# A hand-written opening for a fused pooled-attention and mixture-of-experts kernel

## The chip, the cores and the metric

The kernel runs on one core of one Trainium2 chip. It is one launch; the time is device microseconds of that core. The engines are TensorE (PE in the profile, its weight loads PEld), VectorE (DVE), ScalarE (ACT), GpSimd (POOL) and SyncE (SP), which here issues nearly all transfers. Each engine works through its own instructions in the order in which they stand in its program and waits at an instruction until what it reads is there and what it overwrites has been read.

## The reference, cut to what matters

```python
B, H, S, D = 8, 8, 576, 64                     # q, k, v: [B, H, S, D] f32
k_p = k.reshape(B, H, 72, 8, D).mean(axis=3)   # pooled by 8
v_p = v.reshape(B, H, 72, 8, D).mean(axis=3)
attn = softmax(q @ k_p.T / 8)                  # [B, H, 576, 72]
x = (attn @ v_p) as [4608, 512]                # tokens x (heads, D)
g_idx = argmax(x @ w_group)                    # 4 groups
e_idx = argmax(x @ w_expert[g_idx])            # 4 experts in each
h = maximum(x @ w1[g, e], 0)                   # 512 -> 1024
out = gate_g * gate_e * (h @ w2[g, e])         # 1024 -> 512
```

The routing picks one expert out of 16 for each token; the two gates are the softmax weights of the picks.

## The kernel before

The eight batches go through one after the other, as a software pipeline: while the expert products of batch b run on TensorE, the other engines prepare the attention of batch b+1 and fetch q, k and v of batch b+2. Of each batch one "main" expert is worked on densely for all 576 tokens; the few tokens that went elsewhere are left for a loop behind the last batch. For every batch but the first, the main expert is counted out of the routing. Batch 0 has to start before any routing is known, so its main expert is guessed: `guess_x` (lines 476 to 484) takes the mean of pooled v as a stand-in for x, `guess_e` (line 487 on) multiplies it with the router weights and takes the largest group and expert. The result, `me` (line 471), is read into a register by SyncE, and only then can the eight transfers of that expert's w1 and w2 be issued (line 548).

The order of all instructions is written out by hand in four strings of pieces: `START`, `FIRST`, `STEADY` and `LAST`. `run` (line 916) goes through a string and calls the piece's method, which emits its instructions on their engines in that order. A piece is `who.method:arguments`. The letter a is the attention of the batch at hand, n that of the next, x that of the one after it; m is its experts' part, w the next one's, t a helper. `START` and then `FIRST` are batch 0; nothing else in the program comes before them but the making of constants.

The pieces of the opening, with what they do:

- `load_k:u`, `load_v:u`, `load_r`, `load_q:c`: transfers from HBM; k and v come in two big tiles each (u = 0, 1) and a rest of 64 rows each, which lie in one tile `rem` (v in partitions 0 to 63, k in 64 to 127). q comes in five chunks c of 128 tokens (the last has 64). `load_wr` fetches the router weights, on ScalarE's queue.
- `kr`, `vr`, `rr` (lines 225 to 237): the sums over 8 neighbours, of a k tile, a v tile, the rest. A letter says on which engine: r is one reduction on VectorE, p three additions on GpSimd (line 217 on).
- `kt` and `kta`: transpose pooled k on TensorE, copy it out of PSUM on ScalarE as `kT`. `qt`, `qta`: the same for a chunk of q.
- `sc`, `mx`, `sb`, `ex`, `su_`, `nm`, `pt`: for a chunk, the scores on TensorE (tile `sc`, of which there are two buffers), the row maximum and the subtraction on VectorE, the exponential on ScalarE, the sums and their reciprocal on VectorE, the scaling on GpSimd, the transposition into `pT` on VectorE.
- `rep`, `repa`, `repd`: pooled v repeated along partitions by TensorE, and copied out as `v4` by ScalarE and, masked, as `v5` by VectorE.
- `av:c0:c1`, `ava`, `avd`: the product with v for chunks c0 to c1, and its two copies, a rounded one by ScalarE and the rounding's rest by VectorE (tile `xt`).
- `turn_wr`, `put_wr`: the router weights transposed into `wr`.
- `m.load:1:j`, `m.split:1:j`, `m.spd:1:j`: a quarter j of w1 is fetched, rounded on ScalarE (line 555), and the rounding's rest taken on VectorE (v, line 561) or GpSimd (p, line 565).
- `m.up:f:hf` (line 567): twelve matrix products, one block of 128 columns of w1 with half of the tokens; blocks 2f' and 2f'+1 need quarter f'. `m.ua`, `m.upd` copy it out.
- `t.warm:z` (line 906): z products of a tile of ones with itself, whose result nobody reads.

A tile of a pool with a single buffer, as `rem`, can be filled for the next batch only when its readers are done; SyncE then waits at that transfer, and every transfer behind it in its queue waits too.

Of the kernel before, what the change touches and what calls it, by code (L numbers as in the profile page):

```python
# [46 lines left out]
a.ex:4 m.ua:5:0 n.load_qb:0 a.su_:2 a.nm:2:p a.su_:4 m.ua:3:0 a.nm:4:p m.upd:2:0 a.pt:2 m.split:1:0 a.pt:4 n.rr:r m.ua:4:0 x.load_r:k a.av:2:4  # L47
m.upd:5:0 a.ava:2:2 m.spd:1:3:v a.ava:2:0 n.qb:0 a.avd:2:2 m.upd:3:0 n.kt n.kta m.upd:4:0 a.ava:2:1 n.load_v:0 m.up:6:0 a.ava:2:3 m.up:7:0 n.qb:2
a.avd:2:3 m.ua:7:0 a.avd:2:0 n.sc:2 m.spd:1:0:p m.load:2:3 n.sc:0 a.avd:2:1 n.mx:2 n.sb:2 m.upd:7:0 n.mx:0 n.vr:1:p n.qb:1 x.load_r:v m.ua:6:0
m.load:2:1 m.up:7:1 m.load:2:0 m.split:2:3 n.vr:0 m.up:1:0 m.up:0:0 n.ex:2 n.sc:1 m.upd:6:0 a.rt n.qb:4 m.load:2:2 n.su_:2 n.rep n.sb:0 m.ua:7:1  # L50
m.upd:7:1 x.load_qb:3 n.mx:1 n.nm:2:p m.ua:0:0 n.pt:2 m.spd:2:3:p m.ua:1:0 m.upd:0:0 n.sb:1 m.up:6:1 n.qb:3 m.upd:1:0 n.repa:0 a.route n.ex:0
m.split:2:2 x.load_k:0 x.load_qb:0 m.up:3:1 x.load_k:1 m.ua:6:1 m.ua:3:1 n.ex:1 x.load_v:1 m.split:2:0 n.su_:0 a.count m.up:1:1 n.repa:1 m.up:2:1
m.upd:6:1 n.sc:3 n.repd:1 m.split:2:1 n.sc:4 m.ua:2:1 n.su_:1 m.up:0:1 a.keep_x m.ua:1:1 n.repd:0 n.nm:0:p m.upd:3:1 n.nm:1:p m.upd:2:1 m.spd:2:1:p
m.up:5:1 m.up:4:1 n.mx:4 n.pt:0 m.upd:1:1 n.mx:3 m.spd:2:0:p n.pt:1 m.down:0 n.sb:3 n.sb:4 m.ua:5:1 n.ex:3 m.ua:0:1 n.ex:4 m.ua:4:1 m.upd:5:1
# [906 lines left out]
```

## Time and profile before

| | |
|---|---|
| three runs | 554.21, 553.89, 552.15 us (median 553.89) |
| the profiled execution | 552.38 us, of which its span is 550.7 us |
| instructions | 15235 |
| TensorE busy | 525.7 us (95% of the span) |
| VectorE, GpSimd, ScalarE busy | 360.2, 276.3 and 211.7 us |
| granted TensorE clock, mean of the span | 0.981 |

The page divides the span into 40 slices of 13.8 us. TensorE is busy in nine tenths of nearly every slice; the first has 3 tenths, the second 7 and the third 8, and the last 5. The granted clock, in tenths of full speed, reads 9, 6, 7 in the first three slices, 9 from the fourth to the last but one, and 8 in the last. What the table calls busy is the time in which an instruction was in an engine, whatever clock it had; a product at clock 0.50 counts twice the time of the same product at 1.00.

### The profile page before, as it was taken

The page shows a single profiled execution, that of the slowest core. Times are in us where ns is not written, and L with a number is a line of the kernel's source. Part 1 is how long each engine was busy: PE and PEld are TensorE (multiplying, and loading weights), DVE is VectorE, ACT ScalarE, POOL GpSimd, SP SyncE. Part 2 cuts the span into 40 slices and gives each one's busy share as a digit, 9 for nine tenths or more (in the row PEclk, how much of TensorE's full clock was granted, in tenths as well). Part 3 has the DMA queues.
Part 4 walks back from the last instruction along what each step waited for, and adds up shares of the span by engine and source line. Part 5 has one row for each costly group of instructions (what it writes and reads, how often), then busy time and mean ns, then how long its engine had stood idle before and what let it go on. Part 6 is the DMA issues. An engine that isn't in the chain of part 4 may idle for free.

```text
span 550.7 us, 15235 instructions
## 1 busy us (share of the span) xinstructions
PE 525.7 (95%) x6218; PEld 468.5 (85%) x6218; DVE 360.2 (65%) x940; ACT 211.7 (38%) x402; POOL 276.3 (50%) x259
## 2 busy tenths in 40 slices
PE   3789999999999999999999999999999999999995
PEld 2689987789888998899888998899788988899874
DVE  4788898757755875768755775768756763447520
ACT  2253523445315353355225452354225442344111
POOL 3437386035933578056934578056924554085400
PEclk9679999999999999999999999999999999999998
DMA  9778651591418805492619714496518200544801
...
DMA packets 115649, 81.32 MB, mean 148 GB/s; under 512 B 73562, under 2 KB 92250, under 8 KB 115192
## 3 DMA queue, kind: packets, MB, share of 16 engines
...
## 4 chain that ended last, share of the span: by engine, by line
PE 88%; DMA 4%; DVE 3%; issue 1%; ACT 1%; SPq 1%; POOL 0%; ACTq 0%; POOLq 0%
PE mm L578 36%; PE mm L617 29%; PE sc L374 5%; PE mm L622 5%; PE sc L320 4%; DMA sw<-in_moe_w_dram 2%; PE tp L408 1%; DMA rem<-in_k_dram 1%; DMA ht<-in_moe_w_expert_dram 1%; PE mm L597 1%; PE sc L244 1%; PE mm L910 1%; PE tp L374 1%; DVE su L342 0%; SPq L548 0%
## 5 line engine op out<-in xcount | busy, mean ns | idle before, releaser
L578 PE MATMUL mm<-xt,w 128*128 128x256 f32 (+1 forms) x1536 | 211.7, 297 | 0.9 <-DVE ht L588 0.9
L578 PEld LDWEIGHTS mm<-xt,w 128*128 128x128 f32 x1536 | 205.8, 189 | 3.5 <-ACT ht L583 1.0
L617 PE MATMUL mm<-w,ht 128*128 128x512 f32 x744 | 177.4, 393 | 0.0
L617 PEld LDWEIGHTS mm<-w,ht 128*128 128x128 f32 x744 | 137.9, 188 | 31.2 <-issue 2.5
L565 POOL TENSOR_TENSOR w<-sw,w 128x512 fp32r<-128x512 f32 x94 | 122.6, 1328 | 82.8 <-ACT w L555 80.7
L349 POOL TENSOR_TENSOR p<-p,su 128x576 f32<-128x576 f32 (+1 forms) x40 | 45.8, 1150 | 133.9 <-DVE su L344 126.7
L583 ACT ACTIVATE ht<-mm 128x320 fp32r<-128x320 f32 (+1 forms) x128 | 49.4, 408 | 108.4 <-PE mm L578 108.3
L588 DVE SCALAR_TENSOR_TENSOR ht<-mm,ht 128x256 fp32r<-128x256 f32 (+1 forms) x192 | 60.0, 343 | 39.9 <-ACT ht L583 38.7
L555 ACT CAST w<-sw 128x1024 fp32r<-128x1024 f32 x64 | 66.0, 1043 | 20.5 <-DMA sw<-in_moe_w_dram 16.0
L630 ACT ACTIVATE y<-mm,gm 128x512 f32<-128x512 f32 x31 | 21.3, 687 | 70.0 <-PE mm L617 63.6
L399 POOL TENSOR_TENSOR sw<-xt 128x640 f32<-128x640 f32 (+1 forms) x28 | 40.0, 1463 | 7.2 <-DVE xt L392 7.2
L342 DVE TENSOR_REDUCE su<-p 128x8 f32<-128x576 f32 (+1 forms) x40 | 29.7, 743 | 15.1 <-ACT p L337 15.0
L309 DVE STREAM_TRANSPOSE qT<-q 128x512 f32<-128x512 f32 x35 | 24.6, 702 | 22.7 <-PE sc L320 16.1
L218 POOL TENSOR_TENSOR kv<-kv 128x512 f32<-128x512 f32 x21 | 29.9, 1425 | 10.0 <-DMA kv<-in_v_dram 7.6
L374 PE MATMUL sc<-pT,v 32*64 32x128 f32 (+11 forms) x1560 | 31.0, 290 | 2.6 <-DVE m L493 1.1
L326 DVE TENSOR_REDUCE mx<-sc 128x8 f32<-128x576 f32 (+1 forms) x40 | 29.4, 736 | 6.3 <-PE sc L320 6.3
L355 DVE STREAM_TRANSPOSE pT<-p 128x576 f32<-128x576 f32 (+1 forms) x40 | 30.8, 769 | 3.1 <-POOL p L349 3.1
L337 ACT ACTIVATE p<-p 128x576 f32<-128x576 f32 (+1 forms) x40 | 27.4, 684 | 13.1 <-DVE p L333 8.3
L622 PE MATMUL mm<-w,ht 128*128 128x512 f32 x128 | 32.3, 396 | 0.0
L374 PEld LDWEIGHTS sc<-pT,v 32*64 32x64 f32 (+3 forms) x1560 | 27.4, 139 | 5.6 <-issue 3.2
L561 DVE TENSOR_TENSOR w<-sw,w 128x1024 fp32r<-128x1024 f32 x17 | 24.3, 1428 | 9.2 <-ACT w L555 9.2
L333 DVE TENSOR_TENSOR p<-sc,mx 128x576 f32<-128x576 f32 (+1 forms) x40 | 29.8, 747 | 0.2
(217 smaller groups left out, 480.7 us busy)
## 6 DMA issues: line engine op xcount, KB each, us to landing
...
```

What stands on the lines that cost most here:

```text
L218: add(out=a[..., 0:256], in0=a[..., 0:256], in1=a[..., 256:512], op=ALU.add)
L349: (nc.vector if eng == "v" else nc.gpsimd).tensor_tensor(out=pf, in0=pf, in1=bc(sf, SP), op=ALU.mult)
L355: nc.vector.transpose(out=s.pT[0:n, :, 32 * c:32 * c + 32], in_=s.p[c].rearrange("p u x s -> p (u x s)").rearrange("p (b i) -> p b i", i=3 ...
L374: nc.tensor.matmul(to[64 * x:64 * x + 64], lhsT=w, rhs=s.pT[e, k, 32 * c0:32 * c0 + n], start=(z == 0), stop=(z == 2))
L399: nc.gpsimd.tensor_tensor(out=x, in0=a, in1=b, op=ALU.add)
L555: nc.scalar.copy(out=wh, in_=raw)
L565: nc.gpsimd.tensor_tensor(out=wl[:, p], in0=raw[:, p], in1=wh[:, p].bitcast(F32), op=ALU.subtract)
L578: nc.tensor.matmul(ps[:, 0:n], lhsT=l[:, kc, fs], rhs=xt[:, r, kc, sl], start=(kc == 0 and i == 0), stop=(kc == 3 and i == 2))
L583: nc.scalar.activation(out=s.ht[f][:, o:o + n], in_=s.pu[f, hf][:, 0:n], func=AF.Relu)
L588: stt(out=ht[:, at:at + hi - lo], in0=ps[:, lo - o:hi - o], scalar=0.0, in1=ht[:, lo:hi].bitcast(F32), op0=ALU.max, op1=ALU.subtract)
L617: nc.tensor.matmul(ps, lhsT=s.ht[f][:, 640 * l + o:640 * l + o + 128], rhs=s.w[2, f // 2][r][:, f % 2, :], start=(i == 0), stop=(i == 23))
L622: nc.tensor.matmul(ps, lhsT=s.ht[f][:, 512:640], rhs=s.w[2, f // 2][r][:, f % 2, :], start=(i == 0), stop=(i == 15))
```

## The change

Both strings of the opening, `START` and `FIRST`, are written anew, and three methods learn to do their work in parts. The later strings are as they were. The order within `FIRST` differs only at its beginning.

```diff
 START = """
-a.load_k:1:w a.load_k:0:w a.load_q:0 a.qt:0 a.load_r:k a.load_r:v a.load_q:1 a.kr:0:r a.kr:1:p a.load_v:0 a.load_v:1 a.rr:r a.qta:0 a.load_q:3 a.kt
-n.load_r:v t.load_wr a.kta a.qt:1 a.load_q:4 a.vr:0:r a.sc:0 a.mx:0 t.turn_wr a.qta:1 a.vr:1:p a.sc:1 a.load_q:2 t.warm:2 a.sb:0 n.load_r:k a.ex:0
-n.load_k:0 a.mx:1 t.put_wr a.sb:1 a.su_:0 a.qt:3 a.ex:1 a.rep a.guess_x a.nm:0:p a.su_:1 a.repd:1 a.repa:1 a.nm:1:p n.load_v:1 a.pt:0 a.repa:0 a.qt:2
...
-a.su_:3 t.warm:4 a.nm:3:p a.qta:4 t.warm:7
+t.load_wr t.warm:8 a.load_k:1:w a.load_k:0:w a.load_q:0 a.load_r:k a.load_q:1 a.qt:0 a.kr:0:r a.kr:1:p a.load_r:v a.load_v:0 a.load_v:1 a.qta:0
+a.load_q:3 a.kt a.rr:r:k a.ktail a.kta a.qt:1 a.load_q:4 a.load_q:2 a.rr:p:v a.qta:1 a.sc:0 a.mx:0 a.vr:0:r:0 a.vr:0:p:1 n.load_r:v a.sc:1 a.sb:0
+t.turn_wr a.vr:1:r:0 a.vr:1:p:1 a.ex:0 a.mx:1 t.put_wr a.qt:3 n.load_r:k n.load_k:0 a.sb:1 a.ex:1 a.guess_x n.load_v:1 n.load_k:1 a.su_:0 a.nm:0:p
+a.su_:1 a.rep a.nm:1:p a.pt:0 a.pt:1 a.repd:1 a.repa:1 a.repa:0 a.repd:0 a.guess_e a.qta:3 m.load:1:1 m.load:1:2 m.load:1:3 m.load:1:0 a.av:0:1 a.qt:2
...
+a.sb:3 a.ex:3 n.load_qb:3 n.load_qb:1 a.sc:2 a.mx:2 a.su_:3 a.qta:4
 """
 FIRST = """
-m.split:1:3 a.mx:2 m.up:2:0 n.load_qb:2 m.split:1:2 m.ua:2:0 a.sc:4 a.sb:2 t.warm:8 m.spd:1:2:p m.up:3:0 a.pt:3 m.up:4:0 m.up:5:0 a.ex:2 a.mx:4 a.sb:4
...
+m.up:2:0 a.nm:3:p m.split:1:2 n.load_qb:2 m.ua:2:0 m.up:3:0 a.sb:2 m.spd:1:2:p a.sc:4 m.split:1:3 a.pt:3 m.up:4:0 m.up:5:0 a.ex:2 a.mx:4 a.sb:4 a.ex:4
...
-        def rr(s, eng="r"):
-            s.rp = wk.tile([128, D], F32, name="rp")
-            s.total(s.rp, s.rem, eng)
+        def rr(s, eng="r", part=None):
+            if s.rp is None:
+                s.rp = wk.tile([128, D], F32, name="rp")
+            r = {None: slice(0, 128), "v": slice(0, 64), "k": slice(64, 128)}[part]
+            s.total(s.rp[r], s.rem[r], eng)
...
+            if t is None:
+                s.total(s.vp[:, 2 * u:2 * u + 2, :], s.v[u], eng)
+            else:
+                s.total(s.vp[:, 2 * u + t, :], s.v[u][:, t], eng)
...
+        def ktail(s, ps=None):
+            if ps is None:
+                ps = s.tk2 = ps_m.tile([128, 512], F32, name="mm")
+            for a in range(2):
+                nc.tensor.matmul(ps[64 * a:64 * a + 64, 256:320], lhsT=s.rp[64:128], rhs=ident[64:128, 64:128], start=True, stop=True)
```

So the sum over the rest is now two sums: k's half on VectorE, v's half on GpSimd, and `ktail`, the transposition of the first, is a piece of its own. Each v tile is summed by two engines, one half each. In the program after, lines below 230 stand 5 to 8 lines further down (a score product is L328 and not L320, a product of ones L918 and not L910, an up block L586 and not L578).

On TensorE the program of before begins with these rows (q transposed, k transposed, the k rest, q again, scores of chunk 0, router weights, scores of chunk 1, ones, q):

```order
L298 MATMUL mm<-ident,q 128x128 x4
L273 MATMUL tp<-ident,kp 64x128 x8
L264 MATMUL mm<-ident,rp 64x64 x2
L298 MATMUL mm<-ident,q 128x128 x4
L320 MATMUL sc<-kT,qT 64x72 x16
L900 MATMUL mm<-ident,ht 128x20 x4
L320 MATMUL sc<-kT,qT 64x72 x16
L910 MATMUL mm<-ones 128x128 x2
L298 MATMUL mm<-ident,q 128x128 x4
```

The program of after has in the same place, with eight products of ones in front:

```order
L918 MATMUL mm<-ones 128x128 x8
L306 MATMUL mm<-ident,q 128x128 x4
L277 MATMUL tp<-ident,kp 64x128 x8
L283 MATMUL mm<-ident,rp 64x64 x2
L306 MATMUL mm<-ident,q 128x128 x4
L328 MATMUL sc<-kT,qT 64x72 x32
L908 MATMUL mm<-ident,ht 128x20 x4
L306 MATMUL mm<-ident,q 128x128 x4
```

The router weights' products no longer stand between the scores of chunk 0 and those of chunk 1, and the two products of ones behind them are gone.

Behind the first product with v, TensorE had before (last chunk of q, scores of chunks 3 and 2, ones, one up block, scores of chunk 4, ones, three up blocks):

```order
L298 MATMUL mm<-ident,q 128x64 x4
L320 MATMUL sc<-kT,qT 64x72 x32
L910 MATMUL mm<-ones 128x128 x11
L578 MATMUL mm<-xt,w 128x256 x12
L320 MATMUL sc<-kT,qT 64x72 x8
L910 MATMUL mm<-ones 128x128 x8
L578 MATMUL mm<-xt,w 128x256 x36
```

In the program after these rows read:

```order
L306 MATMUL mm<-ident,q 128x128 x4
L306 MATMUL mm<-ident,q 128x64 x4
L328 MATMUL sc<-kT,qT 64x72 x32
L586 MATMUL mm<-xt,w 128x256 x24
L328 MATMUL sc<-kT,qT 64x72 x8
L586 MATMUL mm<-xt,w 128x256 x24
```

The transposition of q's chunk 2 has come behind the product with v, both groups of ones are gone, and a second up block stands ahead of the last scores. The next row is in both programs the second product with v, `av:2:4`.

On VectorE the sums and the softmax of chunks 0 and 1 stood so before:

```order
L215 TENSOR_REDUCE kp<-w 128x128
L215 TENSOR_REDUCE rp<-rem 128x64
L215 TENSOR_REDUCE vp<-kv 128x128
L326 TENSOR_REDUCE mx<-sc 128x8
L333 TENSOR_TENSOR p<-sc,mx 128x2x4x72
L326 TENSOR_REDUCE mx<-sc 128x8
L333 TENSOR_TENSOR p<-sc,mx 128x2x4x72
```

And after:

```order
L215 TENSOR_REDUCE kp<-w 128x128
L215 TENSOR_REDUCE rp<-rem 64x64
L334 TENSOR_REDUCE mx<-sc 128x8
L215 TENSOR_REDUCE vp<-kv 128x64
L341 TENSOR_TENSOR p<-sc,mx 128x2x4x72
L215 TENSOR_REDUCE vp<-kv 128x64
L334 TENSOR_REDUCE mx<-sc 128x8
L341 TENSOR_TENSOR p<-sc,mx 128x2x4x72
```

The single reduction of v's first tile has become two reductions, of a half of the first tile and a half of the second, and they stand among the softmax steps.

## Rows read from the trace of the kernel before

**Rows 1.** Stretches: start:end, width, busy of PE, PEld, DVE, ACT, POOL, PEclk, DMA
```profile
13.00:16.00 3.00, 0.09 (x1) 0.12 (x2) 2.84 (x3) 0.09 (x1) 1.07 (x1) 0.76 1.26 161
...
21.00:23.00 2.00, 2.00 (x24) 1.81 (x23) 1.89 (x5) 0.15 (x1) 1.59 (x2) 0.91 0.93 293
...
33.00:35.00 2.00, 2.00 (x14) 1.86 (x11) 1.97 (x4) 1.23 (x3) 0.00 (x0) 0.50 0.96 297
35.00:37.00 2.00, 2.00 (x20) 2.00 (x19) 1.90 (x5) 1.07 (x2) 0.76 (x1) 1.00 1.23 291
```

**Rows 2.** The same view, all that comes behind the opening
```profile
60.00:550.70 490.70, 479.72 (x5290) 426.34 (x5282) 315.05 (x849) 189.91 (x358) 247.70 (x215) 1.00 0.48 142
```

**Rows 3.** Chain that ended last, its start: start us, us, what
```profile
2.35 7.28 DMA rem<-in_k_dram
...
9.65 6.12 DMA ht<-in_moe_w_expert_dram
```

**Rows 4.** Timeline, TensorE: start us, us, engine, line, op, out<-in, shapes [idle before <-releaser]
```profile
7.59 1.09 PE L298 MATMUL mm<-ident,q 128*128 128x128 f32 x4 [7.59 <-DMA q<-in_q_dram]
...
15.91 0.63 PE L900 MATMUL mm<-ident,ht 20*128 20x20 f32 x4 [2.93 <-DMA ht<-in_moe_w_expert_dram]
...
18.65 1.06 PE L298 MATMUL mm<-ident,q 128*128 128x128 f32 x4
...
25.68 3.23 PE L374 MATMUL sc<-pT,v 32*64 32x64 f32 x192 [1.12 <-DVE m L493]
...
30.93 2.29 PE L320 MATMUL sc<-kT,qT 64*64 64x72 f32 x64 [1.41 <-DVE xt L392]
...
36.51 1.68 PE L578 MATMUL mm<-xt,w 128*128 128x256 f32 x12
38.11 0.72 PE L320 MATMUL sc<-kT,qT 64*64 64x72 f32 x16
...
45.21 2.55 PE L374 MATMUL sc<-pT,v 32*64 32x96 f32 x192
```

**Rows 5.** Timeline, VectorE
```profile
10.33 1.01 DVE L215 TENSOR_REDUCE rp<-rem 128x64 f32<-128x512 f32 x1 [2.30 <-DMA rem<-in_v_dram]
...
17.78 0.76 DVE L326 TENSOR_REDUCE mx<-sc 128x8 f32<-128x576 f32 x1 [1.90 <-PE sc L320]
18.57 0.76 DVE L333 TENSOR_TENSOR p<-sc,mx 128x576 f32<-128x576 f32 x1
...
24.55 0.29 DVE L261 TENSOR_TENSOR v<-sc,mask 128x128 f32<-128x128 f32 x1 [1.60 <-ACT v L253]
...
25.84 1.16 DVE L497 TENSOR_TENSOR cr<-dg 128x16 f32<-128x16 f32 x1
...
27.45 0.15 DVE L471 TENSOR_SCALAR me<-ct 128x1 int32<-128x1 f32 x1
...
33.78 1.22 DVE L561 TENSOR_TENSOR w<-sw,w 128x1024 fp32r<-128x1024 f32 x1
...
38.88 0.75 DVE L326 TENSOR_REDUCE mx<-sc 64x8 f32<-64x576 f32 x1 [0.67 <-PE sc L320]
...
44.38 0.77 DVE L355 STREAM_TRANSPOSE pT<-p 64x576 f32<-64x576 f32 x1 [0.35 <-POOL p L349]
```

**Rows 6.** Timeline, GpSimd
```profile
14.93 1.26 POOL L218 TENSOR_TENSOR kv<-kv 128x512 f32<-128x512 f32 x1 [7.56 <-DMA kv<-in_v_dram]
...
22.13 1.15 POOL L349 TENSOR_TENSOR p<-p,su 128x576 f32<-128x576 f32 x1 [0.41 <-DVE su L344]
25.70 1.27 POOL L218 TENSOR_TENSOR kv<-kv 128x512 f32<-128x512 f32 x1 [2.42 <-DMA kv<-in_k_dram]
...
38.01 2.50 POOL L565 TENSOR_TENSOR w<-sw,w 128x512 fp32r<-128x512 f32 x2 [0.61 <-ACT w L555]
```

**Rows 7.** Timeline, ScalarE
```profile
32.24 1.04 ACT L555 CAST w<-sw 128x1024 fp32r<-128x1024 f32 x1 [1.75 <-DMA sw<-in_moe_w_dram]
```

**Rows 8.** Timeline, SyncE's queue
```profile
28.64 2.11 SPq L548 DMA_DIRECT2D sw<-in_moe_w_dram x4
```

More of the change, by code (lines that the diff above doesn't have):

```diff
@@ L47 @@
[L47 to L54, printed above, removed]
@@ L55 @@
-m.upd:0:1 n.su_:4 m.spd:2:2:p n.nm:4:p m.upd:4:1 a.gex n.su_:3 n.nm:3:p m.down:12 x.kr:1:p n.pt:4 m.down:13 n.pt:3 n.av:0:4 x.load_qb:2 x.load_qb:1
-n.ava:0:1 x.kr:0:r x.load_v:0 m.down:1 x.rr:r a.gates n.ava:0:4 n.ava:0:0 n.ava:0:3 n.ava:0:2 n.avd:0:4 n.avd:0:0 x.vr:1:p n.avd:0:3 m.da:4 n.avd:0:2
-m.down:2 n.xr:0 m.down:9 n.xr:3 x.kt x.qb:0 n.ava:0:5 n.avd:0:1 n.avd:0:5 x.kta n.xr:2 m.down:6 x.vr:0:r x.sc:0 n.xr:1 n.rt x.rep x.mx:0 x.sb:0
-n.route x.repa:0 x.repd:1 m.down:10 n.main_expert w.load:1:0 x.ex:0 m.da:0 n.gex w.load:1:1 x.su_:0 m.down:11 x.repa:1 w.load:1:3 m.down:3 m.down:4
@@ L59 @@
-w.load:1:2 x.qb:1 x.repd:0 m.down:7 n.gates w.load:2:1 w.split:1:0 m.da:3 w.load:2:0 x.nm:0:p m.down:5 w.spd:1:0:v n.keep_x x.pt:0 w.split:1:1 m.da:1
-m.down:8 m.da:2 w.spd:1:1:v
+m.up:2:0 a.nm:3:p m.split:1:2 n.load_qb:2 m.ua:2:0 m.up:3:0 a.sb:2 m.spd:1:2:p a.sc:4 m.split:1:3 a.pt:3 m.up:4:0 m.up:5:0 a.ex:2 a.mx:4 a.sb:4 a.ex:4
+m.ua:5:0 n.load_qb:0 a.su_:2 a.nm:2:p a.su_:4 m.ua:3:0 a.nm:4:p m.upd:2:0 a.pt:2 m.split:1:0 a.pt:4 n.rr:r m.ua:4:0 x.load_r:k a.av:2:4 m.upd:5:0
+a.ava:2:2 m.spd:1:3:v a.ava:2:0 n.qb:0 a.avd:2:2 m.upd:3:0 n.kt n.kta m.upd:4:0 a.ava:2:1 n.load_v:0 m.up:6:0 a.ava:2:3 m.up:7:0 n.qb:2 a.avd:2:3
@@ new lines @@
+m.ua:7:0 a.avd:2:0 n.sc:2 m.spd:1:0:p m.load:2:3 n.sc:0 a.avd:2:1 n.mx:2 n.sb:2 m.upd:7:0 n.mx:0 n.vr:1:p n.qb:1 x.load_r:v m.ua:6:0 m.load:2:1
+m.up:7:1 m.load:2:0 m.split:2:3 n.vr:0 m.up:1:0 m.up:0:0 n.ex:2 n.sc:1 m.upd:6:0 a.rt n.qb:4 m.load:2:2 n.su_:2 n.rep n.sb:0 m.ua:7:1 m.upd:7:1
+x.load_qb:3 n.mx:1 n.nm:2:p m.ua:0:0 n.pt:2 m.spd:2:3:p m.ua:1:0 m.upd:0:0 n.sb:1 m.up:6:1 n.qb:3 m.upd:1:0 n.repa:0 a.route n.ex:0 m.split:2:2
+x.load_k:0 x.load_qb:0 m.up:3:1 x.load_k:1 m.ua:6:1 m.ua:3:1 n.ex:1 x.load_v:1 m.split:2:0 n.su_:0 a.count m.up:1:1 n.repa:1 m.up:2:1 m.upd:6:1 n.sc:3
@@ new lines @@
+n.repd:1 m.split:2:1 n.sc:4 m.ua:2:1 n.su_:1 m.up:0:1 a.keep_x m.ua:1:1 n.repd:0 n.nm:0:p m.upd:3:1 n.nm:1:p m.upd:2:1 m.spd:2:1:p m.up:5:1 m.up:4:1
+n.mx:4 n.pt:0 m.upd:1:1 n.mx:3 m.spd:2:0:p n.pt:1 m.down:0 n.sb:3 n.sb:4 m.ua:5:1 n.ex:3 m.ua:0:1 n.ex:4 m.ua:4:1 m.upd:5:1 m.upd:0:1 n.su_:4
+m.spd:2:2:p n.nm:4:p m.upd:4:1 a.gex n.su_:3 n.nm:3:p m.down:12 x.kr:1:p n.pt:4 m.down:13 n.pt:3 n.av:0:4 x.load_qb:2 x.load_qb:1 n.ava:0:1 x.kr:0:r
+x.load_v:0 m.down:1 x.rr:r a.gates n.ava:0:4 n.ava:0:0 n.ava:0:3 n.ava:0:2 n.avd:0:4 n.avd:0:0 x.vr:1:p n.avd:0:3 m.da:4 n.avd:0:2 m.down:2 n.xr:0
@@ L61 @@
+m.down:9 n.xr:3 x.kt x.qb:0 n.ava:0:5 n.avd:0:1 n.avd:0:5 x.kta n.xr:2 m.down:6 x.vr:0:r x.sc:0 n.xr:1 n.rt x.rep x.mx:0 x.sb:0 n.route x.repa:0
+x.repd:1 m.down:10 n.main_expert w.load:1:0 x.ex:0 m.da:0 n.gex w.load:1:1 x.su_:0 m.down:11 x.repa:1 w.load:1:3 m.down:3 m.down:4 w.load:1:2 x.qb:1
+x.repd:0 m.down:7 n.gates w.load:2:1 w.split:1:0 m.da:3 w.load:2:0 x.nm:0:p m.down:5 w.spd:1:0:v n.keep_x x.pt:0 w.split:1:1 m.da:1 m.down:8 m.da:2
+w.spd:1:1:v
 """
@@ L263, in kt @@
         def kt(s):
-            tail = lambda ps: [nc.tensor.matmul(ps[64 * a:64 * a + 64, 256:320], lhsT=s.rp[64:128], rhs=ident[64:128, 64:128], start=True, stop=True) for a in range(2)]
             ps = s.tk = ps_t.tile([128, 512], F32, name="tp")
@@ L268, in kt @@
                     nc.tensor.transpose(out=ps[:, 128 * z:128 * z + 128], in_=flat(s.kp[:, 2 * z:2 * z + 2, :]), identity=ident)
-                tail(ps)
+                s.ktail(ps)
                 return
@@ L273, in kt @@
                     nc.tensor.matmul(ps[64 * y:64 * y + 64, 128 * g:128 * g + 128], lhsT=s.kp[:, 2 * (g % 2) + g // 2], rhs=ident, start=True, stop=True)
-            ps = s.tk2 = ps_m.tile([128, 512], F32, name="mm")
-            tail(ps)
+        def ktail(s, ps=None):
[3 more added lines that the diff above has]
+                nc.tensor.matmul(ps[64 * a:64 * a + 64, 256:320], lhsT=s.rp[64:128], rhs=ident[64:128, 64:128], start=True, stop=True)
         def kta(s):
```

6 lines of the change are left out of this document (2 added, 4 removed).

## The prediction

> **What bounds the kernel now.** I read the stretches first. Behind the opening TensorE is busy for 479.72 of 490.70 us at full clock [rows 2]: there the kernel is as long as TensorE's work, the change leaves that work alone, and time can only come out of the opening, or be lost in it. The number that decides is therefore when TensorE starts the second product with v (`av:2:4`), 45.21 us before [rows 4]: the four up blocks that stand ahead of it in both programs are then done, and the rest is the same program.
>
> Next the chain of waits. It goes at the start through two landings: k's rest, issued at 2.35, lands at 9.63, and the router weights, issued at 9.65, land 6.12 us later [rows 3]. TensorE stands for 2.93 us at the products of these weights, until 15.91, and the scores of chunk 1 stand behind them [rows 4]. So VectorE gets chunk 1's maximum only at 17.78 [rows 5].
>
> Then the timelines, for the chain from there to the guess: chunk 1's subtraction ends at 19.33, its scaling on GpSimd runs from 22.13, VectorE waits 1.60 us before the second piece of `v5`, and `me` is ready at 27.60 [rows 5, 6]. SyncE issues the first expert transfer at 28.64, 1.04 later [rows 8], ScalarE's rounding begins at 32.24, 3.6 after the issue [rows 7], VectorE's part ends at 35.00 [rows 5]. The first up block starts at 36.51, behind eleven products of ones [rows 4].
>
> Last the clock. TensorE's granted clock is 1.00 up to some point in 13 to 16 us, in which TensorE is nearly idle, and has a mean of 0.76 there; it is back in 21 to 23, low again at 33 to 35, and 1.00 from 35 on [rows 1]: the levels of 1.2 and 2.4 GHz. The opening is worked off largely at the low one.
>
> **The change part by part**, made against the profiled execution's own time, 552.38 us.
>
> *Router weights first.* Their transfer goes from behind the first copy of q to the first place of ScalarE's queue; it lands long before it is used, and the 2.93 us go. Price: 40 KB in front of k; at the 161 GB/s of 13 to 16 us [rows 1] that is 0.25 us, and I take 0, since VectorE's next tie is v.
>
> *The rest in two halves.* VectorE waited for v's half too and began at 10.33 [rows 5]; k's half landed at 9.63 [rows 3]. That is 0.7 us earlier for kT. Scores of chunk 0 ended before at 12.98 (15.91 less 2.93 [rows 4]), so now at 12.3 to 13.0; I take 12.6.
>
> *v by two engines.* A reduction of 512 columns took 1.01 us [rows 5]. VectorE now does: maximum of chunk 0 (0.76) to 13.4, first half of v to 14.4, subtraction (0.76) to 15.2, second half (v's second tile landed at 14.93 [rows 6]) to 16.2, maximum of chunk 1 to 17.0, subtraction to 17.8. Before it ended at 19.33 [rows 5]: 1.5 us gained. GpSimd's halves have no row; half a tile costs between half and all of the 2.6 us of a whole one (14.93 to 17.5 [rows 6]), so pooled v is complete between 16.2 and 17.5, and either is hidden, since the second scaling comes only after it.
>
> *Guess ahead of the repeated sums.* From chunk 1's subtraction to its scaling it took 2.8 us (19.33 to 22.13 [rows 5, 6]): now 20.6. Scaling 1.15 [rows 6], to 21.75. From the piece of `v5` to `me` VectorE needed 3.05 us (24.55 to 27.60 [rows 5]), which holds the transposition and the choice of the expert; `v5`'s other piece, with twice the columns of the 0.29 us one, is estimated at 0.4. That gives 25.2. The wait of 1.60 us is gone, as `v4` no longer comes between.
>
> In these 3.05 us one addition of 16 columns takes 1.16 us while its neighbour takes 0.15, and GpSimd's sum of 25.70 to 26.97 runs beside it [rows 5, 6]. That sum waits for a transfer (2.42 us idle before it); the transfers are as many as before, so it stays near 25.7 and the guess no longer meets it. So the addition costs some 0.2 and `me` is ready at 24.2; were it slow for another reason, 25.2. I take 24.2, 3.4 us earlier. The Trainium skill, "SBUF — State Buffer", section "Who interferes with whom", says that a VectorE instruction with two SBUF inputs and a GpSimd one that reads SBUF exclude each other; by it 24.2 stands, and without it 25.2 would.
>
> *Up blocks ahead of the last scores, no products of ones.* Issue at 24.2 + 1.04 = 25.25; rounding from 28.85 to 29.9. The product with v starts with `v5` at 23.2 and takes 3.23 [rows 4], 2.5 us earlier than before; scores of chunks 3 and 2, before at 30.93, start at 28.4 and take 2.29 [rows 4], to 30.7. VectorE's maximum (29.5 to 30.3) and its part of the weights (1.22 [rows 5]) end at 31.5. So the first up block starts at 31.5 instead of 36.51. But it starts on the low clock: the eleven products of ones, which before kept TensorE busy from 30.93 until the clock rose at 35.0 [rows 1, 4], are gone. A block took 1.60 us at full clock (36.51 to 38.11 [rows 4]), so 3.2 at half. If the clock rises again 4.1 us after TensorE went to work without a break, at 35.6, then 1.28 blocks are done, the other 0.72 take 1.15, and the scores of chunk 4 start at 36.75, before 38.11. Their maximum starts at 37.5, before 38.88 [rows 4, 5].
>
> Bounds: no rise until both blocks are done, 31.5 + 6.4 = 37.9, maximum at 38.7, gain 0.2. Full clock at once, 34.7; then VectorE is late next. Between the weights' part and this maximum it took 3.9 us (35.00 to 38.88 [rows 5]) and has one subtraction (0.76) more in between, so 36.1: gain 2.8. I take 1.4, the value with the rise that the trace shows.
>
> From that maximum to the last transposition VectorE has the same instructions in both programs, 6.27 us (38.88 to 45.15 [rows 5]). `av:2:4` starts at 43.8 instead of 45.21.
>
> *Products of ones in front.* They lie in the first 7.59 us, in which TensorE waits for q [rows 4]. The four transpositions at 7.59 take 1.09, as at 18.65 on the low clock (1.06) [rows 4]. If the eight products raise the clock, k's transposition is done earlier, and k's rest (above) is late next: between 0 and 0.3 us at the scores, and 0 behind v's second landing. I take 0.
>
> *Sum.* 552.38 - 1.4 = 551.0 on the profiled execution. It lies 1.5 us under the median of 553.89; the four times shown (552.15, 552.38, 553.89, 554.21) have a mean of 553.16, 0.8 above it. I add these 0.8: 551.8.
>
> **Rivals.**
>
> *The clock falls ahead of the second product with v (slower).* Behind the last scores TensorE now has two up blocks only. They need GpSimd's part (2.50 us, before to 40.51 [rows 6], now to about 37.8), take 3.2 and end at 41.0; the product can't start before 43.8. That is 2.8 us of idleness where before eight products of ones and a third block stood. An idle stretch of 2.93 us took the clock down before [rows 1, 4]. A low stretch lasts long: 0.76 in 13 to 16 and 0.91 in 21 to 23 put its ends at 14.6 and 21.4, 6.8 us [rows 1]. In work that TensorE bounds [rows 2] half of that is lost: 3.4 - 1.4 = 2.0 slower, 554.4, with the 0.8 555.2. Against it: the idle stretch has dense work on its left, and the one of 13 to 16 had light work there. It decides if the clock drops between 41 and 46 us. The Trainium skill, "TensorE: Matmul & The Clock Gate", section "HAM oscillation — how this bites in real kernels", warns of just this: idleness between bursts puts the following burst on the low clock; the trace agrees with its 2.93 us, and no run here shows it at this place.
>
> *The up blocks find the clock high, or the chain is quicker.* The gain is then the 2.8 of VectorE's bound: 552.38 - 2.8 + 0.8 = 550.4. For it: TensorE has scores just before. Against: these scores, from 30.93 on, had not raised the clock before 35 [rows 1, 4].
>
> *The order brings nothing (no change).* Two q transfers are now issued earlier, and VectorE waits for v's second tile where GpSimd did. Each 1 us by which this lands behind 15.2 moves everything behind; at 16.6 the 1.4 are gone: 553.2. For it: 7.56 us of GpSimd's waiting was for this tile [rows 6]. Against: the q transfers stand behind it in the queue.
>
> **How the numbers follow.** Forecast 0.43, clock falls 0.25, quick chain 0.17, nothing 0.15. A difference of 0.5%, 2.8 us, is about what a measurement of this kernel tells from no change: faster is below 551.1, slower above 556.7. The forecast lies 0.7 above the first and counts to it with four parts in ten (0.17), the quick chain nearly whole (0.15), the rest with 0.01: 0.33. Slower is the fall of the clock with little gain: 0.07. The same: 0.60. The range reaches from the quick chain's 550.4 less the 1 us by which runs of one program differ from their mean, 549.4, to the falling clock's 555.0.
>
> **What would show it.** No wait of TensorE before the router weights' products, and chunk 1's maximum at 16 to 17 us; `me` at 24 to 25.2; first expert transfer at 25 to 26.5; the first up block at 31 to 32.5, its products twice as long as those before the second product with v; that product at 43 to 44.5, with 2 to 3 us of idleness before it. The forecast is wrong if v's second tile lands behind 16 us, if `av:2:4` starts before 42, or if a stretch behind 43 us shows a clock under 1.00.

## The result, and the profile after

Seven runs of each program on one chip: 556.59 us after (555.0 to 558.51), 553.58 before (551.01 to 555.63). The ratio is 1.0068, its 95% interval 1.0042 to 1.0095: by it the kernel is slower by 0.7%; the medians lie 3.0 us apart. The profiled execution of after took 558.51 us and is the longest of its seven; that of before took 552.38. So the two traces lie 6.1 us apart, and the traces tell where time goes, the ratios how much.

TensorE's timeline of after answers to [rows 4] (start us, us, engine, line, op, out<-in, shapes, count, idle before and its releaser):

```profile
12.15 1.48 PE L328 MATMUL sc<-kT,qT 64*64 64x72 f32 x64
...
24.18 3.41 PE L382 MATMUL sc<-pT,v 32*64 32x64 f32 x192 [2.00 <-ACT v L258]
28.47 1.63 PE L306 MATMUL mm<-ident,q 128*128 128x128 f32 x8 [0.87 <-issue]
30.03 2.20 PE L328 MATMUL sc<-kT,qT 64*64 64x72 f32 x64
...
33.28 5.27 PE L586 MATMUL mm<-xt,w 128*128 128x256 f32 x23 [0.54 <-DVE w L569]
38.48 0.72 PE L328 MATMUL sc<-kT,qT 64*64 64x72 f32 x16
39.13 1.70 PE L586 MATMUL mm<-xt,w 128*128 128x256 f32 x12
...
43.76 1.77 PE L586 MATMUL mm<-xt,w 128*128 128x256 f32 x12 [2.94 <-DVE ht L596]
45.66 4.12 PE L382 MATMUL sc<-pT,v 32*64 32x96 f32 x192
...
50.74 5.22 PE L586 MATMUL mm<-xt,w 128*128 128x256 f32 x24
55.88 1.23 PE L328 MATMUL sc<-kT,qT 64*64 64x72 f32 x64
```

Four things are to be seen. The router weights no longer hold the scores up: all 64 records run in one piece from 12.15. The first up blocks start 3.2 us earlier than in [rows 4], but take 5.27 us for 23 records, and the last scores behind them start 0.37 us later than before, at 38.48. Then TensorE stands still for 2.94 us ahead of up block 5. And from `av:2:4` on (45.66, 0.45 us later than before) each product takes longer: 4.12 us where [rows 4] have 2.55.

The stretches answer to [rows 1] (start:end, width, busy time of PE, PEld, DVE, ACT, POOL, granted clock, DMA share, GB/s):

```profile
13.00:16.00 3.00, 1.21 (x36) 1.03 (x36) 2.97 (x4) 0.53 (x1) 2.69 (x7) 1.00 1.26 199
21.00:23.00 2.00, 1.19 (x6) 1.07 (x6) 1.23 (x3) 0.05 (x1) 0.80 (x1) 0.50 0.96 354
33.00:35.00 2.00, 1.72 (x8) 1.73 (x9) 1.86 (x4) 1.01 (x3) 0.00 (x0) 0.50 1.24 284
35.00:37.00 2.00, 2.00 (x11) 2.00 (x11) 1.45 (x4) 1.85 (x3) 0.96 (x1) 0.50 0.93 86
...
39.00:45.00 6.00, 3.06 (x30) 2.78 (x25) 5.24 (x11) 0.68 (x1) 2.96 (x3) 1.00 0.67 108
...
46.00:55.00 9.00, 9.00 (x218) 8.37 (x203) 5.58 (x11) 3.61 (x10) 7.44 (x8) 0.50 0.79 203
```

At 35 to 37 us, where the clock was 1.00 before [rows 1], it is 0.50. From 39 to 45 TensorE works 3.06 of 6 us; then it is busy without a break from 46 to 55 at clock 0.50, 1.2 GHz. That stretch costs 1.57 us in `av:2:4` (4.12 less 2.55) and 2.09 in the two blocks behind it (5.22; before they took 3.13). From the start of `av:2:4` to the scores behind these blocks it is 10.22 us where it was 6.17, so 4.05 in all. The scores at 55.88 stood at 51.38 before: of the 6.1 us, 4.5 are lost by then; where the rest goes is not followed here. Behind 60 us TensorE is again busy nearly throughout, as in [rows 2]:

```profile
60.00:556.80 496.80, 484.37 (x5403) 430.73 (x5401) 319.69 (x859) 190.75 (x360) 250.44 (x217) 1.00 0.46 140
```

VectorE's timeline answers to [rows 5]:

```profile
17.09 0.76 DVE L341 TENSOR_TENSOR p<-sc,mx 128x576 f32<-128x576 f32 x1
...
24.16 0.29 DVE L266 TENSOR_TENSOR v<-sc,mask 128x128 f32<-128x128 f32 x1 [1.25 <-ACT v L258]
...
24.79 0.17 DVE L505 TENSOR_TENSOR cr<-dg 128x16 f32<-128x16 f32 x1
...
25.41 0.15 DVE L479 TENSOR_SCALAR me<-ct 128x1 int32<-128x1 f32 x1
...
32.01 1.22 DVE L569 TENSOR_TENSOR w<-sw,w 128x1024 fp32r<-128x1024 f32 x1
...
39.24 0.75 DVE L334 TENSOR_REDUCE mx<-sc 64x8 f32<-64x576 f32 x1 [1.24 <-PE sc L328]
...
43.35 0.36 DVE L596 SCALAR_TENSOR_TENSOR ht<-mm,ht 128x256 fp32r<-128x256 f32 x1
```

GpSimd scales chunk 1 from 20.65 ([rows 6]: 22.13), the guess is ready at 25.56 (27.60 before), SyncE issues the first expert transfer at 26.61 ([rows 8]: 28.64), ScalarE rounds from 30.12 ([rows 7]: 32.24), and VectorE's part of the weights ends at 33.2 (35.00 before). All of this is lost again by 39.24, when the maximum of chunk 4 starts, 0.36 us later than before. The last row is what up block 5 waits for: its PSUM buffer is that of block 2, and `m.upd:2:0`, which empties it, stands behind all sums of chunk 4.

### The profile page after: what moved, and what is told of

Read it like the earlier page. It is cut to its first block, busy times and chain, and to the rows that moved or that the text cites. A ratio compares the mean times of both kernels' runs of the same rounds, so it can differ in the third digit from the quotient of the medians.

```text
span 556.8 us, 15189 instructions
## 1 busy us (share of the span) xinstructions
PE 530.9 (95%) x6192; PEld 472.7 (85%) x6192; DVE 360.2 (65%) x941; ACT 211.9 (38%) x402; POOL 278.3 (50%) x265
## 5 line engine op out<-in xcount | busy, mean ns | idle before, releaser
L586 PE MATMUL mm<-xt,w 128*128 128x256 f32 (+1 forms) x1536 | 216.9, 302 | 5.1 <-DVE ht L596 4.4
L586 PEld LDWEIGHTS mm<-xt,w 128*128 128x128 f32 x1536 | 210.3, 194 | 8.6 <-DVE ht L596 3.1
L317 DVE STREAM_TRANSPOSE qT<-q 128x512 f32<-128x512 f32 x35 | 24.6, 702 | 24.2 <-PE sc L328 17.5
L382 PE MATMUL sc<-pT,v 32*64 32x128 f32 (+11 forms) x1560 | 33.0, 302 | 4.2 <-ACT v L258 2.0
L334 DVE TENSOR_REDUCE mx<-sc 128x8 f32<-128x576 f32 (+1 forms) x40 | 29.4, 736 | 9.5 <-PE sc L328 9.5
L382 PEld LDWEIGHTS sc<-pT,v 32*64 32x64 f32 (+3 forms) x1560 | 29.2, 148 | 6.7 <-issue 3.5
L218 POOL TENSOR_TENSOR kv<-kv 128x512 f32<-128x512 f32 (+1 forms) x22 | 29.2, 1326 | 3.4 <-DMA kv<-in_k_dram 3.4
```

Of the source, the lines that this page charges most:

```text
L382: nc.tensor.matmul(to[64 * x:64 * x + 64], lhsT=w, rhs=s.pT[e, k, 32 * c0:32 * c0 + n], start=(z == 0), stop=(z == 2))
L586: nc.tensor.matmul(ps[:, 0:n], lhsT=l[:, kc, fs], rhs=xt[:, r, kc, sl], start=(kc == 0 and i == 0), stop=(kc == 3 and i == 2))
```

## The experiments

Each ratio is taken against the kernel before, run on the same chip in the same set.

| kernel | ratio | 95% |
|---|---|---|
| the change | 1.0068 | 1.0042 to 1.0095 |
| `e1`: ones between blocks 4 and 5 | 1.0059 | 1.0037 to 1.0081 |
| `e5`: the same, second time | 1.0027 | 1.0004 to 1.0050 |
| `e2`: ones ahead of block 2 | 1.0060 | 1.0026 to 1.0094 |
| `e3`: both | 1.0008 | 0.9990 to 1.0027 |
| `e4`: before, router weights first | 0.9992 | 0.9968 to 1.0017 |
| `p1`: new `START`, old `FIRST` | 0.9995 | 0.9978 to 1.0012 |
| `p2`: old `START`, new `FIRST` | 1.0118 | 1.0087 to 1.0149 |
| `p3`: before without its ones | 1.0082 | 1.0055 to 1.0108 |
| `p4`: before, block 3 moved | 1.0022 | 0.9997 to 1.0048 |
| `e6`: the change, `upd:2` early | 1.0109 | 1.0074 to 1.0143 |
| `p5`: `p1`, copies and q earlier | 0.9969 | 0.9950 to 0.9988 |
| `p6`: `p5` with more ones | 1.0029 | 1.0010 to 1.0047 |
| `e7`: the change, no front ones | 1.0065 | 1.0033 to 1.0097 |
| `e8`: `e1`, no front ones | 1.0014 | 0.9992 to 1.0036 |
| `e9`: `e3`, no front ones | 1.0000 | 0.9972 to 1.0029 |
| `p7`: `p5`, no front ones | 0.9965 | 0.9943 to 0.9988 |
| `p8`: `p6`, ones of 64 columns | 1.0133 | 1.0100 to 1.0167 |
| `p9`: `p7` with two ones | 0.9966 | 0.9941 to 0.9990 |

### Is it the clock? Ones put back at either place (e1, e2, e3, e5)

Theory 1: the idle place between blocks 4 and 5 takes the clock down, and that is the loss. Theory 2: the loss is made elsewhere, and the low clock is an accident of the profiled execution. `t.fill:z` issues z products of ones.

```diff
 e1, e3: -a.pt:3 m.up:4:0 m.up:5:0
         +a.pt:3 m.up:4:0 t.fill:11 m.up:5:0
 e2, e3: -a.sc:2 a.mx:2 a.su_:3
         +a.sc:2 t.fill:3 a.mx:2 a.su_:3
```

> The changed kernel with eleven products of ones between the last two up blocks ahead of the second product with v, where TensorE stands for 2.94 us (40.82 to 43.76) in the changed kernel's trace. Theory 1, the clock falls because of that idleness (to 0.50 from 45.2 to 55.4 us) and this is the loss: no stretch under 1.00 behind 43 us, the second product with v takes 2.6 us and not 4.1, and the time falls by 3 to 4.5 us, to 552 to 553.5. Theory 2, the loss is made ahead of 45.7 us (the second product with v starts at 45.66 and not at 45.21) and behind 80 us, and the low clock is one execution's accident: the time stays within 1 us of 556.6.

> The changed kernel with three products of ones ahead of the first up block, in TensorE's gap of 32.2 to 33.3 us; the later gap stays. Theory 1: the clock rises earlier than 38.2 us, the two blocks ahead of the last scores take less than their 5.2 us and the scores come at 36.5 to 38; but the later gap is as long, the clock falls behind it, and the time is 555 to 556.5. Theory 2: what is gained ahead of the last scores is kept: 554.5 to 555.5.

> The changed kernel with both fillings (three products of ones ahead of the first up block, eleven between the last two). Theory 1: no low clock behind 43 us and the second product with v at 43.5 to 45.5 us: 551 to 553, at or under the kernel before. Theory 2: 554.5 to 555.5.

TensorE's timeline of `e1`, then of `e2`, then of `e3`:

```profile
34.69 4.47 PE L586 MATMUL mm<-xt,w 128*128 128x256 f32 x23 [0.54 <-DVE w L569]
...
46.27 2.52 PE L382 MATMUL sc<-pT,v 32*64 32x96 f32 x192 [0.21 <-DVE pT L363]
```
```profile
34.77 3.15 PE L586 MATMUL mm<-xt,w 128*128 128x256 f32 x24
...
43.74 1.88 PE L586 MATMUL mm<-xt,w 128*128 128x256 f32 x12 [1.82 <-DVE ht L596]
45.63 3.68 PE L382 MATMUL sc<-pT,v 32*64 32x96 f32 x192
```
```profile
34.58 3.48 PE L586 MATMUL mm<-xt,w 128*128 128x256 f32 x24
38.00 0.72 PE L328 MATMUL sc<-kT,qT 64*64 64x72 f32 x16
...
46.18 2.61 PE L382 MATMUL sc<-pT,v 32*64 32x96 f32 x192
```

With the place between blocks 4 and 5 filled, `av:2:4` takes 2.52 and 2.61 us, as before; with only the first place filled it takes 3.68, behind 1.82 us of idleness. So in these traces the fall of the clock goes where the idleness goes. And with both places filled the loss is gone, 1.0008. That is as theory 1 had it, and against theory 2, though `av:2:4` of `e3` starts at 46.18 and not at 43.5 to 45.5. But `e1` alone came out at 555.46, where theory 1 said 552 to 553.5; it was run a second time.

> The change with eleven products of ones between up blocks 4 and 5, taken a second time. Open from the first time: its median was 555.5 while its profile showed no fall of the clock and ended early. Theory 1 (without the products of ones ahead of the first up block, the clock falls in some executions at another place, as in the run with those products alone): median 554.5 to 556, and a second profile that shows the up blocks, or the second product with v, at the low clock. Theory 2 (the median of the first time came from what lies behind 60 us): the opening as in the first profile, av:2:4 at 46.3, and time lost behind it.

This time the ratio was 1.0027. The 23 up records, which took 4.47 us in the first trace, took 3.01 in the second: whether the blocks ahead of the last scores find the high clock differs from one execution to the next. With ones ahead of them, 24 records took 3.15 (`e2`) and 3.48 us (`e3`). Both traces start `av:2:4` later than before (46.27 and 45.67). So theory 1 as first put, one idle place and one loss, was too simple: there are two.

### Which half of the change? (p1, p2, p3, p4)

```diff
 p1: START of after, its end as before (t.warm:4, t.warm:7); FIRST of before
 p2: START of before, its end as after (no t.warm:4, t.warm:7); FIRST of after
 p3: before, -t.warm:4 -t.warm:7 -t.warm:8
 p4: before, -m.ua:2:0 a.sc:4 a.sb:2 t.warm:8 m.spd:1:2:p m.up:3:0
             +m.ua:2:0 m.up:3:0 a.sc:4 a.sb:2 t.warm:8 m.spd:1:2:p
```

> The new first string (its end put back as it was before: two groups of ones, a.nm:3 behind a.su_:3, the maximum of chunk 2 in the second string) and the second string of before. Theory 1 (the loss lies in the second part: the ones taken out, so that TensorE stands idle there and its clock falls): faster than before by the router weights' wait that is gone, 551.0 to 552.3; av:2:4 at 43.0 to 44.5 in a run whose clock holds. Theory 2 (the new first part loses too: the v4 copy and the guess stand behind both transpositions of p, q's chunk 2 behind the first product with v): 553.5 to 555.

> The first string of before without its two last groups of ones and with the maximum of chunk 2 and a.nm:3 where the change has them, and the second string of after. Theory 1 (the second part makes the loss): router weights' wait and no ones, so slower than both programs, 556.5 to 559; idleness ahead of up block 5 and a clock of 0.50 behind it. Theory 2 (the loss comes from the new first part): 552.5 to 554.5.

> The kernel before without its 19 products of ones ahead of and behind the scores of chunk 4; the order of the blocks stays one, scores, three. Theory 1 (the ones hold the clock): the first block at the low clock, scores of chunk 4 later than 38.1 or not earlier, TensorE idle behind them, and a time near that of the old front with the new rest, 556.5 to 559.5. Rival (the moved block, which takes the buffer that block 5 waits for and leaves only two blocks behind the scores, makes that loss): 553 to 554.5.

> The kernel before with its second up block moved ahead of the scores of chunk 4, all products of ones kept. Theory 1: the scores of chunk 4 go back by one block at full clock, at most 1.6 us less VectorE's 0.67 of waiting, so 553.5 to 555; idleness of 1 to 2.5 us before block 5 and no fall of the clock, as the ones stand behind the scores. Rival (the moved block makes the loss): 556 to 559, with a stretch at 0.50 behind 45 us.

The second half makes the loss, and in it the ones: the new order of the second string costs 1.2%, taking the 19 ones out of the kernel before and nothing else costs 0.8%, moving the block and nothing else 0.2%, an interval that still holds no change. The new first string alone gives nothing (0.9995), not the 1 to 2 us that theory 1 expected of it. TensorE's timeline of `p2` shows more than idleness:

```profile
45.00 1.69 PE L578 MATMUL mm<-xt,w 128*128 128x256 f32 x12 [2.95 <-DVE ht L588]
46.89 1.84 PE L374 MATMUL sc<-pT,v 32*64 32x96 f32 x130 [0.20 <-DVE pT L355]
50.72 1.55 PE L374 MATMUL sc<-pT,v 16*64 16x96 f32 x62 [1.99 <-issue]
```

In the middle of `av:2:4`, behind 130 of its 192 records, TensorE stands for 1.99 us with nothing to wait for that the profile shows. `p3` has the same gap behind the same 130 records (2.18 us, to 49.34), and in both the clock is low behind it. So the prices of `p2` and `p3` hold this gap besides the missing ones. And the 2.95 us ahead of block 5 are as long as in the change (2.94), yet the clock stays high behind them: 130 records take 1.84 us. It falls only behind the gap. The length of one idle place alone does not tell whether the clock falls.

### Is it the wait for the buffer? (e6)

```diff
-a.ex:2 a.mx:4 ... a.nm:4:p m.upd:2:0 a.pt:2
+m.upd:2:0 a.ex:2 a.mx:4 ... a.nm:4:p a.pt:2
```

> The change with the second copy of up block 2 (on VectorE) ahead of the maximum of chunk 4 and no longer behind its sums, so that block 5 finds its PSUM buffer free. Theory 1 (TensorE's idleness between the scores of chunk 4 and the second product with v takes the clock down, wherever it lies): block 5 follows block 4, 2.5 to 3.5 us of idleness move to behind it, the clock falls all the same, av:2:4 at 45.2 to 46.2, time 555.5 to 557.5. Rival (the wait for the buffer is the loss): 552.5 to 554.5.

```profile
41.26 2.30 PE L586 MATMUL mm<-xt,w 128*128 128x256 f32 x17 [0.27 <-POOL w L573]
46.20 3.02 PE L382 MATMUL sc<-pT,v 32*64 32x96 f32 x192 [2.65 <-DVE pT L363]
```

Block 5 now runs at once, and the idleness moves behind it, 2.65 us ahead of `av:2:4`. The clock falls all the same (0.50 from 48 to 54 us), and the time is 559.69, longer than the 555.5 to 557.5 of theory 1. The buffer only decided where TensorE stood; the rival is out.

### A version that uses the earlier guess (p5), and one with more ones (p6)

```diff
 p5 (on p1): -a.pt:0 a.pt:1 a.repd:1 a.repa:1 ... a.qta:3 ... a.av:0:1 a.qt:2
             +a.repd:1 a.repa:1 a.pt:0 a.pt:1 ... a.qta:3 a.qt:2 ... a.av:0:1
 p6 (on p5): -t.warm:8        +t.warm:20
             -t.turn_wr       +t.turn_wr t.warm:6
```

> As the first of these, and besides the two copies of v4 and v5 ahead of the transpositions of p, and q's chunk 2 turned ahead of the first product with v. Theory 1: the guess is ready 1 us earlier, scores of chunks 3 and 2 at 28.4 to 29.4 where TensorE's clock is high, and the time 549.5 to 551.5, below both programs. Theory 2 (VectorE's chain from those scores to the last transposition sets the end and moves only with the scores' start): the same time as the first of these within 0.8 us.

> The best version so far with twelve more products of ones in front, so that they reach up to the arrival of q, and six behind the router weights' products. Theory 1 (the opening is worked off at the low clock because TensorE has gaps there): clock 1.00 over a part of 8 to 24 us, the guess 0.5 to 2 us earlier, 550 to 551.8. Rival (VectorE's order and the landings of v set the guess, or the light products let the clock fall again): within 0.6 us of the version without them, 551.5 to 552.7.

`p5` is faster than before, by 0.3%, but at 552.06 us not as fast as theory 1 had it (549.5 to 551.5), and its scores of chunks 3 and 2 start at 30.30, not at 28.4 to 29.4. `p6` (554.78, above both ranges) starts `av:2:4` 2.2 us earlier than before and is slower all the same:

```profile
43.04 2.35 PE L382 MATMUL sc<-pT,v 32*64 32x96 f32 x172
47.24 0.45 PE L382 MATMUL sc<-pT,v 32*64 32x64 f32 x20 [1.84 <-issue]
```

The gap named issue again, with clock 0.50 from 49 to 52 us behind it. Counted from the start of the program, the gap stands at the same matmul record as in other kernels. The stretches from 0 to just ahead of a gap give the count in PE's brackets, for after, `p2`, `p6` and the kernel before, one each:

```profile
0.00:28.30 28.30, 18.61 (x348) 16.53 (x349) 18.21 (x43) 7.88 (x16) 14.05 (x35) 0.76 0.82 196
```
```profile
0.00:50.60 50.60, 32.05 (x602) 28.13 (x603) 34.18 (x69) 16.25 (x30) 20.26 (x36) 0.83 0.76 179
```
```profile
0.00:47.10 47.10, 38.72 (x730) 35.35 (x731) 33.32 (x70) 16.23 (x30) 22.50 (x42) 0.89 0.81 193
```
```profile
0.00:144.50 144.50, 127.74 (x1997) 114.57 (x1998) 110.60 (x268) 56.27 (x110) 72.72 (x84) 0.94 0.60 158
```

In every kernel with the new `START` and its front ones of 128 columns, `p6` too, a gap stands at 348. The distances, 254, 128 and 1267, are close to 2, 1 and 10 times 127. The page of after lists a DMA queue of a kind of its own:

```profile
q8 instruction: 50, 0.82, 0.6%
```

These are 50 transfers of 16 KB, about as many as 6,000 records make pieces of 127. Theory 3: TensorE's instructions arrive in pieces of 127 records, each fetched when the one before it is begun; a product with v runs through 127 records in 1.7 to 2.3 us (192 take 2.5 to 3.4), and where it holds a whole piece it is done before the next has come. In `p2` record 475 is passed at 46.9, an instruction transfer starts at 47.5 to 47.75, and the gap ends at 50.72. The Trainium skill, "Runtime: NRT & Kernel Launch", section "Instruction fetch mechanics", says the same of the fetch: blocks of 16 KiB, 256 instructions, the next brought while the current one runs. The trace agrees in the 16 KB, and 127 records, each a weight load and a product, are 254 instructions. The section also says that this is mostly hidden; the 1.84 to 2.18 us here are not.

### The count of records alone (e7, e8, p7, p8, e9, p9)

```diff
 e7 (the change), e8 (e1), e9 (e3), p7 (p5):  -t.warm:8
 p8 (p6): -t.warm:20 ... t.warm:6     +t.warm:40:64 ... t.warm:12:64
 p9 (p7): -t.turn_wr                  +t.turn_wr t.warm:2
```

> The change without its eight products of ones in front (16 matmul records). Theory 3 (TensorE's instructions arrive in pages that end at records 348, 475 and 602, and a product with v which holds the last 127 records before such an end runs into it before the next page is there): the second product with v then covers records 469 to 660, both 475 and 602, so it gets a gap named issue of 1.5 to 2.2 us behind its first 134 records, as with the first string of before and with the kernel without ones; the gap at record 348 in front of q's chunk 2 goes (0.9 us); the clock is low behind both, time 556.5 to 560. Rival (the front ones bring nothing and shift nothing): 555.8 to 557.3, no such gap.

> The change with eleven ones between up blocks 4 and 5, and without its eight ones in front. Theory 3: record 348 lies among the scores of chunks 3 and 2 and no longer behind the first product with v, and the second product with v covers 491 to 682, of which only 602 is an end: no gap named issue at either; scores at 29.0 to 30.0, time 552.8 to 554.8, below the 555.2 to 555.5 with the front ones. Rival: the same 555.0 to 555.8.

> The best version so far without its eight ones in front. Theory 3: the first product with v covers records 145 to 336 and has no gap (1.4 us before), the second covers 507 to 698 and has none; scores of chunks 3 and 2 at 29.0 to 30.0, and 550.5 to 552.0. Rival (the gap is caused by the transfers that run at this time, or the front ones had speeded the opening): gap stays, 552 to 553.5.

> The version with 20 ones in front and 6 behind the router weights' products, each of them cut into two products of 64 columns: the same columns, 52 records more. Theory 3: the first product with v covers records 249 to 440 and the second 611 to 802, with one end of a page each, so both gaps named issue (0.94 and 1.84 us) go, the clock stays at 1.00 behind 49 us, and the time falls from 554.8 to 549.5 to 552. Rival (idleness or transfers decide, the number of records doesn't): 554 to 556, gaps as they were.

> The change with both fillings (three ones ahead of the first up block, eleven between blocks 4 and 5) and without its eight ones in front. Theory 3 (count of records): the gap named issue at record 348, 1.56 us with the front ones, is gone, and the second product with v covers 497 to 688, with one end only; 551.0 to 552.3, at or under before. Rival: as with the front ones, 552.5, or later, if these had helped the opening.

> The best version, with two ones behind the router weights' products in place of eight in front, so that both products with v begin after 148 and 510 matmul records, as in the kernel before. Theory 3: no gap named issue in either, the gaps behind 60 us as in before (2 to 3 us in all), av:2:4 at 43.2 to 44.3, and 551.0 to 552.2. Rival (four records more change nothing): 552.0 to 552.6, as without them.

Up to 60 us the places that theory 3 named came out as it had them, in all six traces. The gap at 348 is gone in `e7`, `e8`, `e9`, `p7` and `p9`, and `p8` has none up to 60 us. `e7` has a new one, behind 135 records of `av:2:4` (134 were expected); it is only 0.21 us long, where 1.5 to 2.2 were expected, in a product that runs at the low clock until 45.7. TensorE's timeline of `e7`, then of `p7`, whose first product with v had a gap of 1.36 us in `p5`:

```profile
29.79 1.41 PE L328 MATMUL sc<-kT,qT 64*64 64x72 f32 x64 [0.66 <-DVE xt L400]
...
44.36 2.47 PE L382 MATMUL sc<-pT,v 32*64 32x96 f32 x135
47.04 0.86 PE L382 MATMUL sc<-pT,v 16*64 16x96 f32 x57 [0.21 <-issue]
```
```profile
23.65 3.23 PE L382 MATMUL sc<-pT,v 32*64 32x64 f32 x192
26.82 0.48 PE L306 MATMUL mm<-ident,q 64*128 64x64 f32 x4
```

The times did so only in part. `e8` lies where it was expected (554.38), below both runs with the front ones, though its interval overlaps that of `e5`. `e7` at 555.87 was expected above 556.5. `e9` at 555.81 was expected at 551.0 to 552.3 and gained nothing that can be told; it has a new gap of 0.84 us at 52.1, at record 730, among the scores behind `av:2:4`. `p7` (552.33, expected 550.5 to 552.0) stays where `p5` was, with 3.9 us of such gaps behind 60 us (before has 2.6). `p8` (561.20) tells nothing of the time: products of half the columns took as long, 17.33 us for 80 records in front, and moved the whole opening by ten us.

`p9` is the best in its trace: `me` at 24.0, `av:2:4` at 42.46, 2.75 us earlier than before. But it meets a gap in the next batch's product (with it, its gaps behind 60 us add up to 3.3, where 2 to 3 were expected), and ends 0.2 us ahead of the profiled execution of before:

```profile
42.46 0.77 PE L382 MATMUL sc<-pT,v 32*64 32x96 f32 x41
...
79.68 1.86 PE L382 MATMUL sc<-pT,v 32*64 32x160 f32 x91 [0.42 <-DVE pT L363]
82.95 0.39 PE L382 MATMUL sc<-pT,v 32*64 32x128 f32 x8 [1.40 <-issue]
```

`p5`, `p7` and `p9` beat the kernel before by 0.3%, and so the changed one too; which of the three is best the runs don't tell.

The gaps also bear on `e3`, whose ones shift the records as well as fill idle places. Summed over a trace, the gaps named issue are 2.6 us before, 3.0 in the change, 3.6 in `e3` and 4.5 to 4.9 in `p2` and `p3`. So `e3` did not get rid of the loss by having fewer of them.

## Why the prediction was wrong

**The step that failed** is "Up blocks ahead of the last scores, no products of ones", the term of 1.4 us, with the maximum of chunk 4 at 37.5 and bounds of 36.1 to 38.7. It started at 39.24, 0.36 us later than before. The two blocks took what the forecast gave them (33.28 to 38.48, against 31.5 to 36.75), but all of them but one record began 1.8 us late, behind VectorE's part of the weights (33.23, forecast 31.5): so the gain was gone. And the loss came from what the term put at nothing. It priced the removal of the ones by the later rise of the clock alone. Their other work, to fill the place behind the last scores in which GpSimd, and then VectorE's sums, hold the blocks back, was left to a rival. There the clock fell, which cost 4.05 us in the trace. `p3` puts the price of taking the ones out of the kernel before at 0.8%, with the gap of 2.18 us in it, and `e3`, with 14 back, is level with before.

**The rival that came true** is the clock that falls ahead of the second product with v, and with it a sign that the prediction itself named: a stretch behind 43 us with a clock under 1.00. The rival's place was nearly right (2.94 us of idleness where it said 2.8, but ahead of block 5 and not behind it; a drop between 41 and 46 us, found at 45 to 46), as was its sign. Its price was too small: it took 3.4 us for the low stretch, from a length of 6.8 us in [rows 1], where this one covers all of 46 to 55 and cost 4.05. It also left 1.4 us of gain standing that were not there, which made 2.0 of the 3.4.

**Also wrong.** The rise of the clock at 35.6 is recorded at 38.4, as the two blocks end. "The wait of 1.60 us is gone" failed: 1.25 us stay, since `v4`'s copy waits on ScalarE for VectorE, whose `v5` now stands behind both transpositions of p. So `me` came at 25.56, not 24.2; `p5`, with the copies ahead, has it at 24.75. The scores of chunks 3 and 2 started at 30.03, not at 28.4: the first product with v began at 24.18 (forecast 23.2) and took 3.41 us (3.23), and from its end to the scores it was 2.44 us (2.02 before). The gap of 0.87 us and the q chunk ahead of the scores explain little of it, for in `e7`, without the gap, the scores wait 0.66 us for VectorE's `xt` and start at 29.79. The maximum of chunk 3 was put 1.1 us behind these scores' start, where it came 1.38 behind in the trace of before (30.93 to 32.31) and 1.30 in that of after. And the front ones, taken at 0, raised nothing that helped (the clock is 0.53 in 7.5 to 11 us), but they shift the records by which that gap falls there.

**The premise** that the start of `av:2:4` decides holds only in part. `e3` starts it 0.97 us later than before and its profiled execution is 0.2 us shorter, `p9` starts it 2.75 us earlier and is also 0.2 us shorter; no low clock lies behind it in either up to 60 us. What comes behind that start differs by more than the gain that was forecast.

**Right.** The router weights' wait is gone, and the change to their transfer alone starts `av:2:4` 1.44 us earlier in its trace (`e4`, below); chunk 1's subtraction ended at 17.85 (17.8 forecast); the addition beside GpSimd's sum took 0.17 us instead of 1.16, GpSimd's sum now starting behind it, at 25.16; the first transfer was issued 1.05 us behind the guess. The Trainium skill, "SBUF — State Buffer", section "Who interferes with whom", has such pairs exclude each other; the trace agrees with its 0.17 us.

```diff
 e4: before, -n.load_r:v t.load_wr a.kta     +t.load_wr ahead of a.load_k:1:w
```

> The kernel before with one edit, the router weights' transfers issued first; all products of ones and the whole order are as before. TensorE's wait of 2.93 us goes. Theory 1 (the loss of the change lies in TensorE's clock, not in its order of loads): chunk 1's maximum comes up to 1.5 us earlier, the first up block up to 1.5 us earlier, no low clock behind 36 us, time 552 to 553.6. Theory 2 (the earlier opening is itself worth nothing): 553.3 to 554.

Measured 551.77 against 552.85, ratio 0.9992: an edit that moves `av:2:4` by 1.44 us in one trace, and that the times can't tell from none.
